# A retention layer with a token and channel mixer on one core: batch 0 multiplies q with its states by row halves, one more transpose of batch 1 goes by crossbar, and k and q are scaled later behind their loads

## The chip, the cores and the metric

The program runs on one NeuronCore of a Trainium2 chip. The metric is device time in microseconds (us) of one launch; the median of three launches of the kernel before is 186.17 us (186.22, 186.17 and 185.26). The engines are TensorE (PE; its weight loads are listed as PEld), VectorE (DVE), ScalarE (ACT), GpSimd (POOL) and SyncE (SP). Each takes its instructions strictly in order.

## What is computed

Two layers follow each other for 4 batches, 768 tokens and 512 channels (8 heads of 64). The first is a recurrent retention with one decay per head, the second a mixer over tokens and then over channels.

```python
for t in range(S):                                   # S = 768, D = 64, H = 8, B = 4
    state = gamma * state + k[:, :, t] (outer) v[:, :, t]
    y[:, :, t] = scale * q[:, :, t] @ state
x  = y as (B, S, H * D)
u  = x + (relu(x^T @ w_tok1) @ w_tok2)^T             # 768 -> 256 -> 768, over tokens
out = u + relu(u @ w_ch1) @ w_ch2                    # 512 -> 1536 -> 512, over channels
```

Inputs and output are float32; inside, the products take float16 and sum in float32.

## The kernel before

The recurrence is done in chunks of 128 tokens (6 chunks). Two heads make a *pair*, so a batch has 4 pairs, and 128 partitions hold the 2 x 64 channels of a pair.

**Front, `front(b, p)`, once for each batch and pair.** k, q and v are loaded by GpSimd's DMA queue (L493, L490), which casts to float16. `decayed` (L531 on ACT, L533 on DVE) multiplies k, and from batch 1 also q, with its decays, one head at a time. `turn` brings k and q into the layout with channels on partitions: by TensorE (L555, L557) and a copy out of PSUM (L565, L570), or by a DMA transpose that SyncE issues (L545), called the crossbar here. The string `TURNS` has three letters for each batch and pair, for k, q and u: `t` is TensorE, `w` is TensorE from a wide load, `x` is the crossbar. The chunk states are k times v (L587), summed over chunks by DVE (L597, L599) and scaled once more into float16 (L617 on ACT, L619 on DVE). Scores are k times q (L638), masked by DVE (L649) and multiplied with v (L669). Then q times the state of the chunk before is added in the same PSUM bank. In the *paired* form (`PAIRED`, all four batches before), the states of both heads lie block-diagonally in a 128 x 128 tile whose other blocks are zero (`cross`, filled by two operations of 64 partitions), and one matmul of 128 rows and 128 columns serves both heads (L695). Here the two PSUM banks hold the two halves of the tokens. The other form, in the code already, keeps the states of a pair in one tile `r`, with head 0 on partitions 0 to 63 and head 1 on 64 to 127, multiplies each head by itself on half of TensorE's rows (L685), and its two PSUM banks hold one head each.

The result is cast to float16 (`x`, L711), goes through the token mixer (L726, relu at L735 or L737, and L746 for the paired form or L751 for the other, which adds to the same banks), is cast again (`u`, L711) and copied in float32 to `X` (L711). u is turned as well, by TensorE (L791, copy at L797) or by the crossbar (L781), into the tile `uT` of its batch.

**Back, `back(b)`, once for each batch.** The channel mixer: batch 0 widens plainly (L825, relu at L841), the others with seven products of half-size blocks instead of eight (L894, with sums on DVE at L864 and L914 and copies at L905). The narrowing (L1047, L1057, L1100 and L973) has copies at L1037 and sums into `X` at L1064 and L982, then stores by SyncE or ScalarE (L1086, L988).

**What sets the order.** The functions only list operations with their dependences. The order in which the engines get them is written down as two tables, `ORDERED` (operation numbers in base 62) and `WAYS` (which of two engines takes it). `arrange` replays that order with a planned cost for each operation, and the replay decides which buffers and PSUM banks an operation gets and how many filler matmuls (L1192) TensorE runs in the first 21 us. An operation's planned costs and its `guard` (a planned distance from what it depends on) therefore act only through the tables and through buffers; at run time an instruction starts when its semaphores allow.

Buffers: 4 each for the loads of k, q and v, so a load waits until the load four before it has been used. GpSimd's queue and SyncE's queue are both first in, first out.

Of the kernel before, what the change touches and what calls it, by code (L numbers as in the profile page):

```python
# [110 lines left out]
def arrange(ops, BANKS, seq, ways):  # L111
# [147 lines left out]
    "0d0106090c070g080e0f000l05031g0a1h0h1k1i1l0j1j0b1u1Q0i1v1w1R1y1U0m1z1S1V1T0k1m1x1n1o0n2u1p1q25241r1B1s0o2q2r"  # L259
    "1t262s0p281A2t1D2v0q30272E29312F1C2G0s1W2I1X321E2H2a1F0u1Y34331Z2J202w212b2x222y0t1G35232z0r2c2d1H2e2A3e2B2f"  # L260
    "1I0w3h2C1L3g2g1J2D1K0v362h2K1M372L2M382N2i390x2O2l3a1N3b3f2P3c4K2j0C3j2Q3d3i3k3m482R0y3l493n3o2k2S3p1O2T2V2m"
    "0A3q1P2n2W2U4a0B3r022o4b2Y3A0z3s2Z3v3t2p3E3u5j3w0F3B4c5k3y3xaf3z4dac3C3FadaP0G3DaM4LaN2Xb1aOb20Daeag3Ob3aQah"
    "3S0EaxaR3RayaY3Qazau3Pav4maw3G4o4e0N3HaZ4f3Iaob03Jb74nb80H4papb93U3KaJ3LaA4g3Mai4h1caqaBaKaC3NaS0IaD4iaE4j1d"
    "aGaFar0Lajas1fak3T3WaL3VaT043XaH4Gal4qaUbd4Hat3Y0MbeaIb41eam3ZanbfaVbm4k4Ibgbo4laW0PbnbhaXb5404J4r18bj0J41b6"
    "bk194244blba0K4s456pbb1a43bq460O1bbObcbi4t4ubrbP4U4vbI0R4M4w4Xbv4N5O4V4x0T5P4O4Pbxbw4Q4y4R4Ybz4SbKbs4T5R4W4z"
    "bt4Cby504Zbp52bB0V5g5fbJ51bA5UbC4A0Q5lbubE4D5m5n4EbTbF4B5obM53bU5V545p5h5W6qc4bX5i5S6rc85q5XbDbN555r5Y47bYbR"
    "5Z56c5c95tbLbS5T6m575v5a5sc7cd5Q585ubV5xce5b5yc65AbWch6n5C5w6o59c07scibZ5z5B0Sc16s4F5Dcm6t6Y6X6u5E0Y5c6v6ZbQ"
    "60cfcn5F6w0U6U61626xcg7t5G6V0W635d5H5J645eca665K676569cj5Icb6b68cc5L6a5M0Xck6c6Acl5N6d156C6y6D706e0Zcq6zcucL"
    "crcvcw6BcM6fcscz6gcQ6EcA6ictcNcRcCcx6hcT71cOcD6GcB6j72cScUcEcJ6l6kd2cV83cG80d0cKcH6WcX7v6F736HcYdRd1136Id3cF"
    "d47u7481dS7y75116Jd78476dWd8dTd5dXdY6Kda7z7wdZdUdbd97A7x6Le07Bdc77e67C6Me1dhbGe7decZbH7Ddie3df85djdd6Ne2e4dk"  # L270
    "78cWcy82d6dA6O7c6QdBe5do796Pdl7bdFdpdC7adGdrcI6R7edmdIdsdqdgdDdJ7d7g6S8y7f10dHdt7hdydKdP7idv14cPdzdLdMdudQdw"
    "7jdEdN16dneWdVeu7k7Eey178zew8B7leXdx86evez7GdOeQ7o877m7JeD8C887HeF7p7IeEeA7r7F7KeH897qeG7nex8A7M7O96eJ8aeBeI"
    "8b7LeS7N8D8e127PeKeM8g7Q6T8c8heU9E8i7ReN8deRf1coe87SeeeVf2c3ea7T998keCec97efeT7U7Wf5eL7Xc28f8m7ZeZ7Ye9ed9ceb"
    "f08E8jeg8F8l7Vf38G9d9a8n9eej9b8H8o9f8Iehf49gf69Fekcpf8ei9h988Jf7en8Kf9eleYePeo8p9Gemfc8Mep8q8L8Q8r8Peq8s8N8u"
    "8t8Ofgfxfdfh9kerfyfl8v9l8SfCfmfefi8w9o8UfDfo9mfnfpfFff8R8T9nfGfzfv8VfjfE9ifqfM8WfA9KfNfsfH9H8Xft9L9jg5fwfJ9I"
    "g6fOfK9J8Yg7ga9MfPg88ZgbfQ8x90fT9q9N9p91fkgdfU929Oge9rfRfW939s9tfVfXgc94fYgkfBg3gf9ug09Pg4gmg1gh9Q9vfZgnggg2"
    "fIglgDgi9wgrfr9SgsgE9A9R9T9x9UgI9ygK9WgJgu9VgofLgLgvgpgt9zgBgMgw9XgFgCgN9ZgSfSgygOgxgTgPgGa19Ya0gzgqhIhCa2hG"
    "gAhE9Ba3hghH9D9ChDhNa4g9gHfuhLhOgjhJhkhMhhhRhKhPgQhFa5gYhQa6hShlhUhigRa8hThrhVgUhphXgV95gZh0a9hshmgWabh1h3hn"
    "hvhoh4esgXhqh5hwh2hth6hjh7huhWh9hxh8aahyhahchYhbi2ijhZi3iRhzikili0i7hBioimi8i4ipa7iqiai1iri5ibi9isiAicihiniH"
    "itiiieivifiCiyiwiBiYhdiSiFizhfiTiDiGiWj8iUiXiIidjfiJiZjriKj0kQiPi6iMj1iQj6iNj3j7jpixigj9ksj4iVjajqkAjdj2jsju"  # L280
    "jektiOjvjbkIjgjtiukJjcjxjhjwjykBjijnj5jzjEjojkiLiEjFjBjlk6jjjAjmkujCkvk2jKk4jDkwk7kKjGkLkxk3kdjIkCkMkekbkykh"
    "jHkzkDkcetjRjLhAjJkffbjSkieOkNjPkgjVkjjQhek5kEkkjTjWfakOkFk8jUkGkPjXjMkHk9kmk0jNkRjYkajOklkSkTknkUkVjZkpkokW"
    "k1kqkXkr"
)
WAYS = (
    "000000000000000000000000000000000000000000000000000000000000000000000000000000010000010000000000000000000100"
    "000001000000010000000000000000000000100001010000010000010000000000000001001001000000000000100000000000000000"
    "001000100000010000010000000001101000000011000000000000000000000000000000000100000100000000000000000000000000"
    "010000000000000000000000000000000000000110010000000000000000000000000001010000000000000000000010000000001101"
    "000100001000000000000000000000100000010000000000000000000000000011001001000000000000000000000000001100000100"  # L290
    "000000000000000000100000000010010000000000000001000000000000001001000000000000000000000000000000000000000000"
    "000000000000000000000000000000000000000000000000000000000000000000000000000011000000000000000000000000000000"
    "000000000000010000000000000000000000000000000010000000000000000100000000010000000001000000100000000010000000"
    "000000000000000000000000000000001100000000000000000000110000000000000000000011000000000000000100101000010000"
    "000001000000101000000000000000000000000100000010100000001000000000000000000000000000000000000000010000000000"
    "000000000011000000000010001000000100000000000000000000000001010000000001000000000000000000000100000010010000"
    "000000010100000000010000001000000000010000000000000001000001000010001000110000010000000100000000000000000000"
    "0000"
# [4 lines left out]
def kernel(  # L303
# [39 lines left out]
    PAIRED = (0, 1, 2, 3,)  # L343
# [3 lines left out]
    TURNS = "twt twt twt twt twx twx twt twt xxx xxx xxx xxx xxx xxx xxx xxx".split()  # L347
# [31 lines left out]
    def one(eng, cost, emit):  # L379
        return [(eng, cost[0], cost[1], emit)]  # L380
# [7 lines left out]
    lnG = const_p.tile([P, H], FP, name="lnG")  # L388
    lnsc = const_p.tile([P, 1], FP, name="lnsc")
# [10 lines left out]
    def prep(eng, cost, emit, deps=(), prio=(-20, 0, -1), takes=(), uses=()):  # L400
        return Op(ops, prio, [(eng, cost, cost + 40, emit)], deps, takes, uses)
# [15 lines left out]
    gy_op = prep("ACT", 190, lambda: nc.scalar.activation(gy, lgs, AF.Exp, bias=lnsc, scale=1.0), [lgs_op])  # L417

# [18 lines left out]
    gq_op = prep("ACT", 2450, emit, [since_op, lnh_op, logs_op], (-20, 0, -1, 1), [LATE], [SINCE])  # L437
# [64 lines left out]
    def front(b, p):  # L502
# [22 lines left out]
        def decayed(tag, src, dep, g, hard):  # L525
            dst, got = Slot(tag), []
            for j in range(2):
                def emit(e, j=j):
# [170 lines left out]
        else:  # L699
            y2 = [op(one("PE", (145, 310), emit), rs + [kt, qt, y0], [], [QT, RS] + Y, tiled="row")]  # L700
# [524 lines left out]
```

## Time and profile before

| | |
|---|---|
| median of three launches | 186.17 us |
| the profiled execution, whole | 186.5 us |
| its span, first to last instruction | 184.7 us |
| TensorE busy | 176.6 us (96%), 2088 matmuls |
| VectorE busy | 168.9 us (91%) |
| ScalarE busy | 137.6 us (74%) |
| granted TensorE clock | 1.000 |
| DMA queue of GpSimd (q0) | 13.18 MB, its packets 91.1% of the 16 engines' span |

The first row of the page gives the span; the time of a launch is that and 1.8 us around it. A row of the timeline is: start, duration, engine, line, operation, output and input names, shapes, and in brackets the idle time before it and what ended that. The shape `128*64 128x64` of a matmul is rows times columns of the weights and then the moving operand. Matmuls are pipelined, so the duration of one matmul is longer than the step from one to the next; the step is read from the starts in the timeline, or from the chain of waits, where `0.67 PE bank L746 x12` is twelve matmuls in 0.67 us. In the rows by windows, each engine has its busy microseconds with the number of instructions, then the granted clock, the number of DMA engine microseconds per microsecond and GB/s.

### The profile page before, as it was taken

To read this page: it belongs to the slowest core of one execution; us is meant where nothing else is said; L and a number is where in the kernel's file an instruction comes from. 1 tells how busy PE (TensorE), PEld (TensorE's weight loads), DVE (VectorE), ACT (ScalarE), POOL (GpSimd) and SP (SyncE) were. 2 spreads that over 40 slices of the span, in tenths; PEclk is the share of its full clock that TensorE was granted. 3 is DMA by queue.
4 is the path that set the end of the run, shared out by engine and by line. 5 is a ranking of instruction groups with operands and counts; after the bars stand their busy time and mean duration, and the time that the engine had idled before them with its cause. 6 is when DMAs were issued, how large, how long until landed. Compare 5 with 4: busy or idle time off the path is not lost.

```text
span 184.7 us, 5303 instructions
## 1 busy us (share of the span) xinstructions
PE 176.6 (96%) x2088; PEld 134.2 (73%) x2088; DVE 168.9 (91%) x446; ACT 137.6 (74%) x323; POOL 53.9 (29%) x63
## 2 busy tenths in 40 slices
PE   7698899999999999999999899999999999999992
PEld 3356698666789988866678798767769986566892
DVE  2799999789999999999999989999999999889993
ACT  5749899857899699999999687798996335786010
POOL 8995776454462108604053200000000000000000
PEclk9999999999999999999999999999999999999999
DMA  6999999999999999999999997604002261100296
GB/s 116 150 164 188 180 185 197 186 197 201 165 157 154 146 157 132 130 153 145 119 224 142 133 253 142 169 0 85 5 0 46 68 188 57 62 0 0 84 378 225
DMA packets 94137, 25.31 MB, mean 137 GB/s; under 512 B 83616, under 2 KB 91296, under 8 KB 94112
## 3 DMA queue, kind: packets, MB, share of 16 engines
q0 software_dynamic: 67728, 13.18, 91.1%
q1 hardware_dynamic: 24944, 9.90, 27.7%
q10 hardware_dynamic: 1440, 1.90, 2.9%
q8 instruction: 16, 0.26, 0.6%
q14 instruction: 9, 0.07, 0.2%
HBM read 26.74 MB, written 6.29 MB: 179 GB/s over the span
## 4 chain that ended last, share of the span: by engine, by line
PE 67%; issue 11%; POOL 11%; DMA 9%; ACTq 0%; ACT 0%; DVE 0%; POOLq 0%
PE bank L894 15%; PE bank L1047 14%; PE bank L1057 9%; PE bank L825 9%; DMA v<-in_v_dram 5%; PE bank L746 4%; DMA k<-in_k_dram 4%; PE bank L726 4%; POOL k L493 3%; PE bank L973 3%; POOL v L493 3%; PE bank L669 2%; PE bank L638 2%; POOL q L490 2%; POOL q L493 2%
## 5 line engine op out<-in xcount | busy, mean ns | idle before, releaser
L649 DVE TENSOR_TENSOR am<-bank,mask 128x384 f16<-128x384 f32 x64 | 32.5, 547 | 1.5 <-PE bank L638 1.3
L914 DVE TENSOR_TENSOR h<-bank,us 128x384 f16<-128x384 f32 x54 | 28.6, 549 | 2.1 <-ACT us L905 1.4
L493 POOL DMA_DIRECT2D v<-in_v_dram x16 | 16.4, 1028 | 38.7 <-PE bank L695 15.1
L905 ACT COPY us<-bank 128x384 f32<-128x384 f32 x50 | 22.9, 483 | 5.3 <-PE bank L894 3.7
L894 PE MATMUL bank<-hs,late 128*128 128x384 f16 x108 | 22.7, 326 | 0.0
L1037 ACT COPY us<-bank 128x256 f32<-128x256 f32 x27 | 10.1, 377 | 14.6 <-PE bank L1047 13.3
L1047 PEld LDWEIGHTS <-hs 128*128 128x128 f16 x192 | 18.1, 98 | 2.9 <-issue 0.8
L1064 DVE TENSOR_TENSOR X<-X,bank 128x256 f32<-128x256 f32 (+1 forms) x45 | 17.8, 407 | 1.4 <-PE bank L1057 1.0
L894 PEld LDWEIGHTS <-late 128*128 128x128 f16 x144 | 13.1, 98 | 7.3 <-DVE hs L864 0.3
L599 DVE SCALAR_TENSOR_TENSOR U<-U,gp,bank 128x64 f32<-128x64 f32 x64 | 16.9, 274 | 0.9 <-ACT U L597 0.2
L1047 PE MATMUL bank<-wsum,hs 128*128 128x256 f16 x132 | 17.6, 273 | 0.0
L825 PE MATMUL bank<-uT,wc 128*128 128x384 f16 x96 | 17.6, 326 | 0.0
L617 ACT ACTIVATE cross<-U,gp 64x320 f16<-64x320 f32 x28 | 15.7, 559 | 2.5 <-DVE U L599 2.0
L493 POOL DMA_DIRECT2D k<-in_k_dram x15 | 15.4, 1029 | 4.0 <-ACT kT L570 2.0
L894 PE MATMUL bank<-uT,wc 128*128 128x384 f16 x72 | 16.5, 326 | 0.0
L711 ACT CAST u<-bank 128x384 f16<-128x384 f32 x28 | 13.4, 482 | 3.3 <-PE bank L746 3.2
L746 PE MATMUL bank<-h,wt 128*128 128x128 f16 x192 | 15.2, 219 | 0.1
L711 ACT COPY X<-bank 128x384 f32<-128x384 f32 x31 | 14.7, 489 | 0.4 <-DVE u L711 0.4
L894 PEld LDWEIGHTS <-wc 128*128 128x128 f16 x108 | 9.9, 98 | 5.7
L726 PE MATMUL bank<-x,wt 128*128 128x128 f16 x192 | 13.4, 219 | 0.6 <-DMA wt<-in_moe_w_tok_dram 0.5
L711 ACT CAST x<-bank 128x384 f16<-128x384 f32 x28 | 13.0, 492 | 1.2 <-PE bank L695 1.2
L746 PEld LDWEIGHTS <-wt 128*128 128x128 f16 x192 | 12.3, 98 | 2.1 <-DMA wt<-in_moe_w_tok_dram 0.2
(94 smaller groups left out, 390.0 us busy)
## 6 DMA issues: line engine op xcount, KB each, us to landing
out_dram<-X SPq DMA_DIRECT2D x16, 256.0 KB, 2.6
q<-in_q_dram POOLq DMA_DIRECT2D x16, 192.0 KB, 8.0
v<-in_v_dram POOLq DMA_DIRECT2D x16, 192.0 KB, 7.9
k<-in_k_dram POOLq DMA_DIRECT2D x15, 192.0 KB, 8.8
wc<-in_moe_w_ch_dram POOLq DMA_DIRECT2D x5, 512.0 KB, 13.8
out_dram<-X ACTq DMA_DIRECT2D x6, 256.0 KB, 2.7
wc<-in_moe_w_ch_dram POOLq DMA_DIRECT2D x2, 256.0 KB, 10.5
us<-in_k_dram SPq DMA_DIRECT2D x1, 384.0 KB, 3.5
```

Source lines behind the costliest of these rows:

```text
L493: (nc.sync if hard else nc.gpsimd).dma_start(out=tile_of(s, [P, 2, NC, D], FP if hard else F16), in_=src.rearrange("h (c p) d -> p (h c) d ...
L599: nc.vector.scalar_tensor_tensor(out=u[:, c], in0=u[:, c - 1], scalar=gp[:, p:p + 1], in1=st, op0=ALU.mult, op1=ALU.add)
L649: nc.vector.tensor_tensor(am, SC[g].tile[:, :m * P].rearrange("p (i t) -> p i t", t=P), mask.to_broadcast([P, m, P]), ALU.mult)
L711: (nc.scalar.copy if e == "ACT" else nc.vector.tensor_copy)(tile(), t)
L726: nc.tensor.matmul(acc[:, jt * P:(jt + 1) * P], wt1[:, i, jt * P:(jt + 1) * P], X16.tile[:, i].rearrange("p h d -> p (h d)"), start=(i == ...
L746: nc.tensor.matmul(Y[j].tile[:, 2 * i * D:2 * (i + 1) * D], wt2[:, jt, t], H1.tile[:, jt], start=False, stop=(jt == NJ - 1), skip_group_ch ...
L825: nc.tensor.matmul(acc[:, :SH], wc1[:, ct, ft * P:(ft + 1) * P], UT.tile[:, ct, sh * SH:(sh + 1) * SH], start=(ct == 0), stop=(ct == NP - 1))
L894: nc.tensor.matmul(acc[:, :SH], left(ct), r[:, ct], start=first and ct == 0, stop=ct == C2 - 1, skip_group_check=True)
L905: (nc.scalar.copy if e == "ACT" else nc.vector.tensor_copy)(ks[:, j], R1.tile[:, :SH])
L914: nc.vector.tensor_tensor(h(m, sh), R.tile[:, :SH], KS.tile[:, j], ALU.add)
L1047: nc.tensor.matmul(acc_[:, lo], l[:, j], r[:, j], start=first and j == 0, stop=j == K2 - 1, skip_group_check=True)
L1064: (nc.vector if e == "DVE" else nc.gpsimd).tensor_tensor(dst(), dst(), b_(), ALU.add)
```

## The change

- `PAIRED` loses batch 0. Its four pairs now take the form with one head per PSUM bank: the states are scaled by one operation of 128 x 320 (`r`, L609 or L611 of the changed file) where two of 64 x 320 stood; q times states is 10 matmuls of 64 rows and 64 columns per pair, on the two halves of the rows, where 5 of 128 rows and 128 columns stood; the second product of the token mixer is 24 matmuls with 64 moving columns per pair where 12 with 128 stood; the casts have the shape 6 x 64 where they had 3 x 128 or 384.
- `TURNS`: u of the third pair of batch 1 goes by the crossbar and not by TensorE.
- `decayed`: the first of the two scalings of k or q of batches 1 to 3 has a planned distance of 1200 ns behind its load.
- ScalarE gets one activation of 128 x 1 (`warm`) ahead of the four that make the decays of q, so its table load moves to this one.
- Two planned costs differ (a DVE scaling of the one float32 k load, q times states by row halves).
- `ORDERED` and `WAYS` are written anew for all of it.

```diff
 ORDERED = (
-    "0d0106090c070g080e0f000l05031g0a1h0h1k1i1l0j1j0b1u1Q0i1v1w1R1y1U0m1z1S1V1T0k1m1x1n1o0n2u1p1q25241r1B1s0o2q2r"
+    "0e0107080d050h090f000g060c031h0m0a0i1l1i0b0n1j1m1k0j1P1v1Q0k1z1T1u1U1R0l1n1S1w1y1o0o2r1x231p222s0p2n1q272o1r"
...
-    PAIRED = (0, 1, 2, 3,)
+    PAIRED = (1, 2, 3,)
...
-    TURNS = "twt twt twt twt twx twx twt twt xxx xxx xxx xxx xxx xxx xxx xxx".split()
+    TURNS = "twt twt twt twt twx twx twx twt xxx xxx xxx xxx xxx xxx xxx xxx".split()
...
+    warm = const_p.tile([P, 1], FP, name="warm")
...
+    warm_op = prep("ACT", 190, lambda: nc.scalar.activation(warm, lnsc, AF.Exp), [logs_op])
...
-    gq_op = prep("ACT", 2450, emit, [since_op, lnh_op, logs_op], (-20, 0, -1, 1), [LATE], [SINCE])
+    gq_op = prep("ACT", 2450, emit, [since_op, lnh_op, logs_op, warm_op], (-20, 0, -1, 1), [LATE], [SINCE])
...
-                got.append(op(either(emit, ACT=(506, 610), DVE=(340, 420) if hard else (600, 690) if b == 0 else (231, 312)),
+                got.append(op(either(emit, ACT=(506, 610), DVE=(580, 660) if hard else (600, 690) if b == 0 else (231, 312)),
                               [dep, gy_op if tag == "q16" else g_op], [] if got else [dst], ([dst] if got else []) + [src],
                               behind=got[-1] if got else None))
+                if b > 0 and j == 0:
+                    got[0].guard = 1200
...
-            y2 = [op(one("PE", (145, 310), emit), rs + [kt, qt, y0], [], [QT, RS] + Y, tiled="row")]
+            y2 = [op(one("PE", (175, 343), emit), rs + [kt, qt, y0], [], [QT, RS] + Y, tiled="row")]
```

Line numbers of the changed file are 2 higher than before for nearly all lines after L417. How the tables move instructions is shown at three places; names with a number are buffers (`k_2162` is a load, `k_22_2299` the scaled copy of it, `bank_...` a PSUM bank).

First, TensorE in batch 0, the pair whose token mixer comes first. Before, one of five matmuls of q with the states and one of twelve of the second product of the mixer:

```order
L695 LDWEIGHTS qT_173
L695 MATMUL bank_298<-cross_77,qT_173 128x128
L746 LDWEIGHTS wt_81
L746 MATMUL bank_328<-h_56_484,wt_81 128x128
```

and now two of ten, one for each head, on TensorE's two row halves:

```order
L687 LDWEIGHTS qT_183
L687 MATMUL bank_323<-r_36_331,qT_183 128x64
L687 LDWEIGHTS qT_183
L687 MATMUL bank_324<-r_36_331,qT_183 128x64
```

The states come from one tile `r` and go to a bank for each head.

Second, SyncE's queue from its first crossbar on, which is in batch 1. Before:

```order
L545 DMA_TRANSPOSE qT_1428<-q_24_1163 128x6x128
L781 DMA_TRANSPOSE uT_1457<-u_62_1141 128x6x128
L545 DMA_TRANSPOSE qT_1490<-q_25_1294 128x6x128
L545 DMA_TRANSPOSE kT_1516<-k_23_1242 128x6x128
L545 DMA_TRANSPOSE kT_1554<-k_21_1498 128x6x128
L781 DMA_TRANSPOSE uT_1457<-u_63_1357 128x6x128
L545 DMA_TRANSPOSE qT_1622<-q_24_1601 128x6x128
L781 DMA_TRANSPOSE uT_1875<-u_61_1827 128x6x128
```

and now:

```order
L547 DMA_TRANSPOSE qT_1477<-q_24_1333 128x6x128
L783 DMA_TRANSPOSE uT_1503<-u_62_1131 128x6x128
L547 DMA_TRANSPOSE kT_1521<-k_23_1398 128x6x128
L547 DMA_TRANSPOSE qT_1549<-q_25_1492 128x6x128
L547 DMA_TRANSPOSE kT_1590<-k_21_1406 128x6x128
L783 DMA_TRANSPOSE uT_1503<-u_63_1438 128x6x128
L783 DMA_TRANSPOSE uT_1503<-u_61_1586 128x6x128
L547 DMA_TRANSPOSE qT_1934<-q_24_1620 128x6x128
```

In the sixth and seventh place stand u of the second and of the third pair of batch 1 (`uT_1503`); the q that stood seventh now comes behind both.

Third, ScalarE in the narrowing of batch 1, where the last loads of k and q are scaled. Before:

```order
L711 COPY X_1848<-bank_2106 128x3x128
L531 ACTIVATE k_22_2299<-k_2162,gk 128x6x64
L1037 COPY us_2211<-bank_2178 128x256
L711 CAST x_55_2341<-bank_2311 128x384
L711 CAST x_55_2341<-bank_2289 128x384
L617 ACTIVATE cross_77<-U_2238,gp 64x5x64
L531 ACTIVATE k_21_2364<-k_2137,gk 128x6x64
```

and now:

```order
L713 COPY X_1910<-bank_2155 128x3x128
L1039 COPY us_2377<-bank_2348 128x256
L531 ACTIVATE k_21_2385<-k_2019,gk 128x6x64
L531 ACTIVATE k_22_2289<-k_1755,gk 128x6x64
L713 CAST x_55_2421<-bank_2361 128x384
L531 ACTIVATE q_25_2427<-q_2236,gy 128x6x64
L713 CAST x_55_2421<-bank_2391 128x384
```

Before, the k load that is scaled here is the third of the last five of GpSimd's queue:

```order
L493 DMA v_2121<-in_v_dram 128x12x64
L493 DMA k_2137<-in_k_dram 128x12x64
L493 DMA k_2162<-in_k_dram 128x12x64
L493 DMA q_2185<-in_q_dram 128x12x64
L493 DMA v_2339<-in_v_dram 128x12x64
```

and now both k loads stand ahead of the v load that opens the last burst, and two q loads follow it:

```order
L493 DMA k_2019<-in_k_dram 128x12x64
L493 DMA v_2195<-in_v_dram 128x12x64
L493 DMA q_2213<-in_q_dram 128x12x64
L493 DMA q_2236<-in_q_dram 128x12x64
L493 DMA v_2418<-in_v_dram 128x12x64
```

So the load that a scaling on ScalarE follows most closely is a k load before (`k_2162`) and a q load now (`q_2236`).

More of the change, by code (lines that the diff above doesn't have):

```diff
@@ new lines @@
+    "0q2p1s251A1t2Z262q1B0r241C2V302B2A2W0u2F1V2C1W2X1D2E0s2Y2t1X1Y2u1E1Z282v29202w212D0w1F2x2y2z2a1G380t2b3b392c"
+    "3a1H0z1K3c1I2d3d1J0x2G1L2H2e2I312J2i0y322f332K343x1M352L2g360D372j3e2h2M3g0A3f2N3t3u3y1N3h2Q0v3i2l2O2k3j2P2R"
+    "0C3v3k2T1O0B3w3l3o3m2m3z4D3A0H3p3n5b452U3q3r2Sa73sa43BaE3C0G4Ea5aHa6a8aF3Da9aI3E0F5caGaTaUaJ3H023Faj0EaV3Jak"
+    "3Iamalan3K3G3Maa41423LaKaoaL460J04ab43ac3Nap44aq0I1daBar3O3PaCaM4f0QaD473Q4jay3Raz484iaW4z4gaX3S1eaY0Nbb3T4h"
+    "bcaAag493U4a4AaZ3V3X4k4bah3Y4c0Kad1gaib04das1fb1aeat3W4BafaN3Z4eb54C0Mb6au19avb7aw4mb80U1baxb9bdaO1abGaP0Lba"
@@ new lines @@
+    "4lb2bH4ob31c574N0Ob44F4P4n4Gbi4R4p0SbeaQaRbfbj4qaSbg0Tbn4H4r4O5Jbk4Ibhbo584S4QbrbAbpbs4J4K4T4vbq4L0PbwbC4M5G"
+    "bt6e5Hbx4Ubl4sbu4W4VbW5d4t5M4XbBbL4u5K4wbm4Y5L5Nbv4xbE5e6h5fc0bM404Z5g5ObP5hc1bXbF5I596i5Pc55i5a5QbQbJ6j5R5j"
+    "bZ50bDbK5l6f5kbN515m6gc6535nbOc97k5o4y5q6P5p5sbSbY5u545rca5tbT0W6k565vbRce6l55bI5w520Rcf5S6mc76n5x0X5T6o5U6p"
+    "c85y5W0V5B5z5Vc25C5X175Z5Y5D61cb5Ac363186062cc5Ec4646scd5F0Z656v6qci1466cjcm6ucDcn6ackcEco6Mcr6N6tcIcs6w6710"
+    "cJcKcpcu68clcLcvcFcMctcB69cw6Q6ScUcN6TcCcy6RcGcP6bczcS6rdL6U6O7lcVcWcQdJ6ccZ6VcTcX6xdK6y7mcA6z6Ad07n0Y7qdM6B"
@@ new lines @@
+    "dO6W7rd26CdN6X15dQdP7scOd17td3dRcq7S7o6Dd4dS7ud97TcYdTd67UdadYdU6EdVd7dZdb7v6Y6F7pdWdc70cH7V6Zds74dgbUdt716I"
+    "6Gdi7Wd8dxdh7X72ddcx73djdydude6H756ddAdkdvdzd5dl77dqdBdX7679dm78dCdn116JdHdrdDdEdo7aeO16cRdIdwdFdf7bem6K12eq"
+    "8qePeo7c7yerdpendG7Y7d8Y7AeveI7Z8rex7z7e8s80ew7g7C7wesep7x6L81ez827heteMey7i7B7jeA7DeB7f83eKeNeE9weubyeC8Z7E"
+    "cgeJ7F8613ch7HeF7G8t90e0eR877IeTe1eS8u7JeD848v88eV7KeU85e68abze27LbV7Oe7eX899291e4e3eWeL7M8c8eeY8w7N94eQ7Peb"
+    "eZ8xe57R8b7Q8dece9958f8y96ef8z8g938Aea97f0e8eged8B988Cf18h99eef48E8ieh9a8j8G8Dei8I8k8H8m8lf88Ffpf5f99cfqejfd"
@@ L299 @@
+    "000100000000000000100000000000000000000000000010000000000000000100001000000100100000000000000001010000100001"
+    "00000010000000000010010000000000001000000000010000000000100010000100000100000001000000010000000000000001"
 )
```

55 lines of the change are left out of this document (18 added, 37 removed).

## The prediction, made before the changed kernel ran

> **What bounds the kernel now.** I read the rows by windows first, to see which engine is full in which stage, then TensorE's waits, then the chain of waits.
>
> ```profile
> 20.00:32.00 12.00, 11.85 (x234) 10.47 (x232) 11.22 (x29) 10.81 (x26) 8.96 (x11) 1.00 1.69 187
> 32.00:52.00 20.00, 20.00 (x207) 13.20 (x205) 18.39 (x36) 15.57 (x36) 9.01 (x10) 1.00 1.74 185
> 76.00:103.00 27.00, 26.90 (x313) 19.62 (x312) 26.77 (x74) 25.86 (x65) 9.05 (x9) 1.00 2.11 155
> 103.00:117.00 14.00, 13.17 (x187) 11.68 (x184) 13.27 (x37) 10.89 (x28) 1.01 (x1) 1.00 0.97 184
> 117.00:151.00 34.00, 34.00 (x366) 26.38 (x365) 32.74 (x81) 25.25 (x63) 0.00 (x0) 1.00 0.25 58
> ```
>
> From 20 us on TensorE (the first busy number) is full in every stage but one: 0.15 us idle from 20 to 32 us, 0.10 from 76 to 103, 0.83 from 103 to 117. So from 20 us the time is TensorE's list of matmuls plus its few waits. From 76 to 103 us VectorE (26.77 of 27) and ScalarE (25.86) are nearly as full: a wait on either there reaches TensorE almost undiminished. What opens that stretch, and its one large wait:
>
> ```profile
> 19.59 0.62 PE L726 MATMUL bank<-x,wt 128*128 128x128 f16 x8 [0.54 <-DMA wt<-in_moe_w_tok_dram]
> 103.23 0.51 PE L638 MATMUL bank<-qT,kT 64*128 64x128 f16 x12
> 104.54 0.81 PE L1047 MATMUL bank<-wc,hs 128*128 128x256 f16 x6 [0.80 <-ACT us L1037]
> 101.26 0.86 ACT L711 COPY X<-bank 128x384 f32<-128x384 f32 x2
> 103.62 0.61 ACT L531 ACTIVATE k<-k,gk 128x384 f16<-128x384 f16 x1 [1.50 <-DMA k<-in_k_dram]
> 104.14 0.35 ACT L1037 COPY us<-bank 128x256 f32<-128x256 f32 x1
> 96.45 7.14 DMA k<-in_k_dram
> ```
>
> The first real product of the token mixer waits for its weights until 19.59 us; before that TensorE runs fillers. At 102.1 us ScalarE has done its copies and stands 1.50 us before a k load that lands at 96.45 + 7.14 = 103.59. Behind it in its queue is the copy L1037 that TensorE's product needs.
>
> **The change part by part, against the span of 184.7 us.** The matmuls, by the steps of the chain:
>
> ```profile
> 29.48 0.67 PE bank L746 x12
> 58.22 0.35 PE bank L669 x12
> 53.15 0.28 PE bank L695 x5
> 53.43 0.44 PE bank L638 x12
> 53.87 0.28 PE bank L587 x10
> 27.13 0.34 PE bank L791 x6
> ```
>
> *Token mixer of batch 0.* Per pair 12 matmuls of 128 columns (0.67 us, 56 ns each) become 24 of 64. The nearest row is L669, the same 128 x 128 weights with 64 columns: 0.35 / 12 = 29 ns, so 0.70 us. Four pairs: 4 x (0.70 - 0.67) = +0.12 us. The bound above is 56 ns each: 4 x 0.67 = +2.7 us; I take the row of the same shape.
>
> *q times states of batch 0.* Five matmuls (0.28 us) become ten of 64 rows and 64 columns on alternating row halves. L638 alternates row halves too: 12 of 128 columns in 0.44 us; if two ran one after the other it would be 12 x 56 = 0.67, so two overlap (0.34) and 0.10 goes to the change of form. Ten of half the columns then take 10 x 29 / 2 + 0.10 = 0.25 us, and L587 (ten on column halves) took 0.28. Without overlap it is 0.29 + 0.10 = 0.39. So the bounds are 4 x (0.25 - 0.28) = -0.1 and 4 x (0.39 - 0.28) = +0.4; I take 0.
>
> [...]
>
> *u of the third pair by crossbar.* TensorE loses six transposes (L791): -0.34 us. A copy of uT leaves ScalarE or VectorE. SyncE gains one transpose, priced below.
>
> *States scaled once.*
>
> ```profile
> L617 ACT ACTIVATE cross<-U,gp 64x320 f16<-64x320 f32 x28 | 15.7, 559 | 2.5 <-DVE U L599 2.0
> L619 DVE TENSOR_SCALAR cross<-U,gp 64x320 f16<-64x320 f32 x4 | 2.2, 540 | 0.1
> L436 ACT ACT_TABLE_LOAD x1 | 1.3, 1283 | 2.2 <-DVE lnh L430 2.2
> ```
>
> An operation's length goes with its elements per partition, so one of 128 x 320 takes about the 0.56 us of one of 64 x 320: four times 0.55 us leave ScalarE and VectorE. In the window from 20 to 32 us they have 11.22 and 10.81 of 12 us of work, but TensorE idles there only 0.15 us, so at most that is won. Against it, the casts x of a pair can now both start only when all ten matmuls are done, where the first half could go ahead; TensorE's list has another pair's matmuls in between (q times states, scores, the mixer of the pair before, over 1 us together) and two casts take 0.9. I count 0, with 0.4 either way.
>
> *Table load.* It waits 2.2 us now; the 128 x 1 activation needs less and pulls it and the decays forward by under 1 us. The weights that land at 19.59 hide that: before them TensorE has the same real matmuls in both lists (four pairs' transposes, three pairs' scores). Without that cover it would be worth under 1 us. Worth 0.
>
> *The margin.* The k load of the wait now stands ahead of the last burst in GpSimd's queue and is long there, and its scaling is not followed by TensorE's next copy. The gap at TensorE goes: L638 starts at 103.23 and needs 0.44, the next product at 104.54, so -0.87 us.
>
> *What may be late next.* In-order ScalarE and SyncE now stand before other transfers. The rows that price them:
>
> ```profile
> 69.49 1.28 SPq L781 DMA_TRANSPOSE uT<-u  x1
> 70.88 1.28 SPq L545 DMA_TRANSPOSE qT<-q  x1
> uT<-u SPq DMA_TRANSPOSE x1, 5.7
> qT<-q SPq DMA_TRANSPOSE x1, 7.4
> 69.82 1.09 POOL L493 DMA_DIRECT2D v<-in_v_dram  x1 [8.92 <-PE bank L587]
> 70.90 2.04 POOL L493 DMA_DIRECT2D q<-in_q_dram  x2
> q<-in_q_dram POOLq DMA_DIRECT2D x1, 192.0 KB, 7.7
> k<-in_k_dram POOLq DMA_DIRECT2D x1, 192.0 KB, 9.2
> 77.39 1.19 PE L894 MATMUL bank<-uT,wc 128*128 128x384 f16 x6
> 94.44 1.01 POOL L493 DMA_DIRECT2D v<-in_v_dram  x1 [8.37 <-PE bank L695]
> 97.56 1.03 POOL L493 DMA_DIRECT2D q<-in_q_dram  x1
> ```
>
> (a) The widening of batch 1 needs all of uT. The third pair's u is cast on ScalarE behind two scalings, by my count of the list at 69.4 us; its crossbar goes out at 69.5, where the one of 69.49 took 5.7 us: it lands at 75.2. TensorE's first product of that widening came at 77.39; six transposes (0.34) fewer and ten matmuls of another pair (0.28) that now follow it make that about 76.8. Cover 1.6 us; behind the product stand all of TensorE's matmuls. If it goes out one crossbar later (70.8) and takes 7.4 us, it lands at 78.2 and costs 1.4; with the 9.2 us of the slowest load of that burst, 3.2.
> (b) In the burst of loads that starts at 69.82 the second is now a k whose scaling stands behind two copies of that widening (turn about 78.0). A second load took 7.7 us from 70.90, to 78.6: 0.6 us late. But the transposes that shared the DMA engines then ran until 70.88 + 7.4 = 78.3, and SyncE now has none in that place until about 80 us. I take on time.
> (c) The last burst: v at about 95.0, then two q, the second at 97.1, landing by the k's 7.14 us at 104.2; ScalarE's turn comes behind the cast of x after 104.1, at 104.5. Between 0 and the old 0.9 us.
> Together 0 to 0.6 + 0.9 with (a) in cover, up to 4.7 if all are late; I take +0.1, since each has cover, if little.
>
> *Sum.* 184.7 + 0.12 + 0 - 0.34 + 0 - 0.87 + 0.1 = 183.7 us of span. With the 1.8 us around it, 185.5 against the profiled 186.5; that execution was 0.3 above the median of 186.17, so I forecast **185.2 us**.
>
> **Rivals.**
> *B, the wait only moves.* ScalarE stands before the second q of the last burst, (c), or the k of (b), and loses the 0.9 us again: 185.2 + 0.9 = 186.1. For it: cover of 0.3 us and less, and a burst of loads still opens when a v buffer comes free. Against it: the load that decides has the v and one q ahead of it and no k, and ScalarE's turn is by my count behind its landing.
> *C, the third u comes late (slower).* The crossbar between 67 and 78 us now carries k, u, u with the loads of batch 2 in flight; TensorE stands still before L894. Price 1.4 to 3.2; between the two, landing at 78.9, 2.1: 185.2 + 2.1 = 187.3. It decides from 76.8 us on; below that it costs nothing, and at about 77.8 it has eaten the gain. For it: 5.7 and 7.4 us side by side in the rows. Against it: the slower one shared with q and v loads as well as a transpose ahead.
> *D, a fixed price per matmul.* If the 64-column matmuls of batch 0 step at 56 ns, +2.6 to the sum: 187.8. L669 speaks against it.
> *E, the order does more.* What I count at 0 comes in: 0.4 at the casts of batch 0, 0.1 at q times states, the 0.25 us of idle time before 103 us, and nothing is late (0.1): 185.2 - 0.85 = 184.3.
>
> **Chances.** Forecast 0.52 (0.36 of it faster by over 0.5%, 0.16 within), B 0.21 (0.02 faster, 0.18 within, 0.01 slower), C 0.17 (0.01 within, 0.16 slower), D 0.03 (slower), E 0.07 (faster). So faster 0.45, within 0.5% 0.35, slower 0.20; 0.5% is 0.93 us, about what a measurement of this kernel tells from no change. The range of 8 in 10 goes from just below E, 184.2, to C's 187.3; the forecast's own is 184.6 to 185.9.
>
> **What would show it.** Right: batch 0's mixer step (24 matmuls) 0.70 us and q times states 0.25 to 0.28; TensorE's first product of the mixer still at 19.6 after the weights; no idle over 0.3 us at the copies L1039 around 104 us; the crossbar of the third u landed before TensorE's first L896 (L894 before); k loads of batch 3 long there when ScalarE reaches them. Wrong: TensorE idle at L896 with a DMA of uT as what ended it (C), ScalarE idle before L531 on q or k by a DMA (B), steps of 50 ns and more at L753 (D), or a wait in a place that I haven't priced, as batch 0's casts.

## The result, and the profile after

Six launches of the changed kernel took 188.92 us in the median (188.71 to 189.24), six of the kernel before on the same chip 185.48 (185.26 to 186.22): a ratio of 1.017, 95% interval 1.014 to 1.019. The change makes the kernel 3.4 us slower where 185.2 us, a little faster, was forecast. The profiled launch took 189.0 us with a span of 187.2.

The first row of the page on the engines, for the changed kernel:

```profile
PE 178.1 (95%) x2151; PEld 134.3 (72%) x2151; DVE 170.5 (91%) x447; ACT 134.7 (72%) x318; POOL 53.5 (29%) x63
```

TensorE has 2151 matmuls where it had 2088: 68 more in batch 0, six transposes fewer, one filler more. Its rows by windows (columns as before: TensorE, its weight loads, VectorE, ScalarE and GpSimd busy, clock, DMA share, GB/s):

```profile
20.00:32.00 12.00, 10.26 (x263) 9.03 (x261) 9.70 (x23) 8.89 (x22) 9.25 (x11) 1.00 1.65 189
32.00:52.00 20.00, 20.00 (x224) 13.59 (x224) 17.26 (x36) 14.49 (x34) 10.52 (x11) 1.00 1.78 184
76.00:103.00 27.00, 26.37 (x302) 18.39 (x300) 26.76 (x73) 26.03 (x65) 9.62 (x10) 1.00 1.90 159
103.00:117.00 14.00, 14.00 (x189) 12.60 (x187) 13.93 (x40) 11.58 (x29) 1.01 (x1) 1.00 1.25 205
```

The list of TensorE's waits from 20 to 184 us (us in total, times, longest):

```profile
PE bank L557 <- issue: 1.0, 1, 1.0
PE bank L728 <- issue: 0.8, 1, 0.8
PE bank L640 <- DVE X L1066: 0.4, 1, 0.4
```

The hole of 0.83 us at 103 to 117 us is gone, as forecast. A new one stands from 20 to 32 us: 10.26 us busy of 12, where it was 11.85, although more matmuls run there (263 against 234). VectorE and ScalarE are less busy there than before (9.70 and 8.89 against 11.22 and 10.81), so neither is the bound, and TensorE's two waits have the releaser "issue": it stood for nothing that the profile names. The timeline shows where:

```profile
19.40 0.84 PE L728 MATMUL bank<-x,wt 128*128 128x128 f16 x12 [0.33 <-DMA wt<-in_moe_w_tok_dram]
23.51 0.87 PE L753 MATMUL bank<-h,wt 128*128 128x64 f16 x24
24.31 0.53 PE L557 MATMUL bank<-ident,q 128*64 128x128 f16 x12
24.77 0.34 PE L728 MATMUL bank<-x,wt 128*128 128x128 f16 x3
25.89 0.68 PE L728 MATMUL bank<-x,wt 128*128 128x128 f16 x9 [0.78 <-issue]
26.68 0.32 PE L687 MATMUL bank<-r,qT 64*128 64x64 f16 x10
26.93 0.35 PE L663 MATMUL bank<-v,am 128*128 128x64 f16 x6
...
30.80 0.23 PE L557 MATMUL bank<-ident,q 128*64 128x128 f16 x2
31.98 1.14 PE L557 MATMUL bank<-ident,q 128*64 128x128 f16 x34 [0.96 <-issue]
```

Both stands are in the middle of a series of equal matmuls, after the 3rd of 12 products and the 2nd of 36 transposes, which have no semaphore between them. Counted in TensorE's instructions (each matmul is a weight load and a product), the 706th and the 962nd come first after a stand: 256 apart. The page has two rows of packets that carry instructions. One (q14) has 9 packets of at most 8 KB. The other, of the kernel before and then of the changed one (queue, packets, MB, share of the 16 engines):

```profile
q8 instruction: 16, 0.26, 0.6%
```

```profile
q8 instruction: 17, 0.28, 0.6%
```

Each of these packets is 16,384 bytes in the trace. Putting a border at instruction 193 + 256 n, so that both stands fall on one, there are 16 borders in the 4,190 instructions of the kernel before and 17 in the 4,317 of the changed one: a packet for each border. Read from the trace (us):

```
kernel    border   first instruction   its packet   later by   block before     stand at
          at no.   behind it starts    starts                  it used up in    the border
before     449        20.71             23.67        2.96         8.54             -
before     705        27.41             30.19        2.78         6.70             -
before     961        35.84             38.24        2.40         8.43             -
changed    449        20.18             23.52        3.34         8.78             -
changed    705        25.89             29.51        3.62         5.71            0.99
changed    961        31.98             35.82        3.84         6.09            1.18
```

The stand is counted here from the start of the last matmul ahead of the border to the start of the first one behind it. A packet takes 0.9 to 1.0 us here. I read this so: in these stages the next block of instructions is asked for when TensorE enters the present one, and its transfer starts 2.4 to 3.8 us later. The trace shows the packet and not the asking; late in the program, with few loads (DMA share 0.25 from 117 to 151 us), some packets of the changed kernel start up to 1.3 us before the first instruction behind their border does (148.44 against 149.73), so the asking may be somewhat earlier than the entry. Where TensorE stands, it goes on 1.5 us behind the end of the packet (23.52 + 0.89 = 24.41, then 25.89; 29.51 + 0.89 = 30.40, then 31.98), 5.7 and 6.1 us after it entered the block before. In the thirteen stands of 0.5 us and more of the changed kernel and the runs below, the 1.5 us are 1.2 to 1.6. The kernel before used its blocks up in 6.70 us and more and never noticed. The changed one needs 4.7 and 4.9 us (5.71 less 0.99, 6.09 less 1.18) and stands for the rest. This is theory F.

**Where the 3.6 us of span are.** For each matmul I take its start less the place it would have if TensorE never waited (steps of 29, 56, 110 and 163 ns for 64, 128, 256 and 384 columns, from 0.35 us for twelve in L669, 0.67 for twelve in L746, 0.66 for six in L1047 and 1.95 for twelve in L825 in the chain of the kernel before; half of it on row and column halves, where L638 has 0.44 for twelve and L587 0.28 for ten; 0.1 us at a change of form, an estimate from L638; all from the first token product on). TensorE's lag behind its list, in us:

```
                              at 33   77     92    103    134   end
before, run again  (E1)        0.56  0.93   1.38   1.40   1.47  1.47
changed                        2.40  2.86   3.55   4.50   4.74  4.82
t2 of batch 0 in halves (E2)   1.69  2.14   3.01   3.08   3.12  3.12
changed, batch 0 paired (E4)   0.78  1.24   1.95   2.88   3.15  3.20
before, batch 0 unpaired (E7)  2.23  2.77   3.25   3.70   3.71  3.73
changed, exchange (E9)         2.37  2.80   3.55   4.47   4.71  4.79
changed, fillers cut (E12)     1.57  2.05   2.75   3.68   3.96  4.01
```

Changed against before: 1.84 us more up to 33 us, 0.33 from there to 92, 0.93 from 92 to 103, 0.25 behind: 3.35 in all. The list itself is 0.29 us shorter (159.02 against 159.31), it starts 0.15 later, and the time behind the last matmul is 0.40 longer: 3.61 us, the 187.2 against 183.6 of span. The steps are round prices: with 0.1 us at every change of the rows or columns of the weights, the four shares are 1.97, 0.34, 0.94 and 0.24 us and the list is 0.44 us shorter, so the split is good to some 0.15 us. The 0.33 and the 0.25 us were not taken apart.

### The profile page after: what moved, and what is told of

It is laid out like the page before. It is cut to its first block, busy times and chain, and to the rows that moved or that the text cites. A ratio compares the mean times of both kernels' runs of the same rounds, so it can differ in the third digit from the quotient of the medians.

```text
span 187.2 us, 5429 instructions
## 1 busy us (share of the span) xinstructions
PE 178.1 (95%) x2151; PEld 134.3 (72%) x2151; DVE 170.5 (91%) x447; ACT 134.7 (72%) x318; POOL 53.5 (29%) x63
## 3 DMA queue, kind: packets, MB, share of 16 engines
q10 hardware_dynamic: 1440, 2.23, 3.3%
## 4 chain that ended last, share of the span: by engine, by line
PE 81%; POOL 5%; DMA 5%; DVE 4%; issue 2%; ACT 2%; POOLq 0%; DVEq 0%
PE bank L896 20%; PE bank L1049 15%; PE bank L1059 11%; PE bank L827 8%; PE bank L728 5%; DMA wt<-in_moe_w_tok_dram 5%; PE bank L748 4%; PE bank L640 3%; PE bank L975 3%; PE bank L671 2%; PE bank L697 2%; PE bank L753 2%; POOL k L493 2%; PE bank L589 2%; POOL q L490 2%
## 5 line engine op out<-in xcount | busy, mean ns | idle before, releaser
L907 ACT COPY us<-bank 128x384 f32<-128x384 f32 x51 | 23.4, 485 | 8.3 <-PE bank L896 4.7
L1039 ACT COPY us<-bank 128x256 f32<-128x256 f32 x26 | 9.6, 374 | 11.5 <-PE bank L1049 10.2
L713 ACT CAST x<-bank 128x384 f16<-128x384 f32 x31 | 14.7, 492 | 1.2 <-PE bank L697 1.0
L843 ACT ACTIVATE h<-bank 128x384 f16<-128x384 f32 x24 | 11.0, 486 | 4.5 <-PE bank L827 4.4
L1059 PEld LDWEIGHTS <-h 128*128 128x128 f16 x132 | 12.5, 98 | 1.8
L713 ACT COPY X<-bank 128x384 f32<-128x384 f32 x28 | 13.5, 495 | 0.3 <-DVE u L713 0.3
L728 PEld LDWEIGHTS <-wt 128*128 128x128 f16 x192 | 11.7, 98 | 2.6 <-issue 0.9
```

The lines of the kernel that those rows point to most:

```text
L713: (nc.scalar.copy if e == "ACT" else nc.vector.tensor_copy)(tile(), t)
L728: nc.tensor.matmul(acc[:, jt * P:(jt + 1) * P], wt1[:, i, jt * P:(jt + 1) * P], X16.tile[:, i].rearrange("p h d -> p (h d)"), start=(i == ...
L907: (nc.scalar.copy if e == "ACT" else nc.vector.tensor_copy)(ks[:, j], R1.tile[:, :SH])
L1059: nc.tensor.matmul(acc_[:, lo], l[:, j], r[:, j], start=first and j == 0, stop=j == K2 - 1, skip_group_check=True)
```

## The experiments

All times are medians beside runs of the kernel before on the same chip. F is the theory above; the other letters are named in the expectations, and B to E in the prediction (rival E is not one of the runs E1 to E12).

**E1, the kernel before once more.**

> The kernel before, unchanged, profiled once more. The forecast took 0.87 us out for a wait at 103.2 to 104.5 us that stood in the one profiled execution (186.5 us); the median of six executions of this kernel is 185.48. Theory W (the wait belongs to the kernel): it is there again, near 0.8 us, and the span is 184.7. Rival (the wait is an accident of that execution): it is missing or shorter, the span is near 183.7 to 184.0, and removing it was worth little from the start.

185.36 us, span 183.6, and no wait of TensorE over 0.2 us from 20 us on. ScalarE in that execution:

```profile
100.94 0.86 ACT L711 COPY X<-bank 128x384 f32<-128x384 f32 x2
102.00 0.61 ACT L531 ACTIVATE k<-k,gk 128x384 f16<-128x384 f16 x1 [0.20 <-DMA k<-in_k_dram]
102.52 0.35 ACT L1037 COPY us<-bank 128x256 f32<-128x256 f32 x1
```

The k load landed at 102.0 us, not at 103.59; the copy L1037 behind the scaling came at 102.52, not at 104.14, and the 0.87 us are not there. The rival holds: the wait comes and goes with the landing of one load.

**E2, instructions alone, in the kernel before.**

```diff
                     for jt in range(NJ):
-                        nc.tensor.matmul(Y[j].tile[:, 2 * i * D:2 * (i + 1) * D], wt2[:, jt, t], H1.tile[:, jt],
-                                         start=False, stop=(jt == NJ - 1), skip_group_check=True)
+                        for g in range(2 if b == 0 else 1):
+                            c0, c1 = (g * D, (g + 1) * D) if b == 0 else (0, 2 * D)
+                            nc.tensor.matmul(Y[j].tile[:, 2 * i * D + c0:2 * i * D + c1], wt2[:, jt, t],
+                                             H1.tile[:, jt, c0:c1], start=False, stop=(jt == NJ - 1),
+                                             skip_group_check=True)
```

> The kernel before with one edit: the second token product of batch 0 as 96 matmuls of 64 columns where 48 of 128 stand, same banks, same result. Theory F (TensorE's instructions arrive in blocks of 256, a block every 6 us or so while the loads run): the blocks that the kernel before uses up in 6.70 us are then used up in some 5.4 to 5.8 us, so TensorE stands at two places between 24 and 34 us, for nothing that the profile names, 256 instructions apart, and the time rises by 0.6 to 1.8 us. Rival P (the price list of the forecast: 29 ns for 64 columns): plus 0.1 us, no stand. Rival D (a fixed price of 56 ns for a small matmul): plus 2.6 us, spread over the 96 matmuls, no stand.

187.64 us against 186.33, ratio 1.009 (1.005 to 1.013). One stand, not two, at instruction 961:

```profile
30.20 1.14 PE L555 MATMUL bank<-ident,q 128*64 128x128 f16 x34
32.32 0.25 PE L555 MATMUL bank<-ident,q 128*64 128x128 f16 x2 [0.97 <-issue]
```

The 48 more matmuls cost a stand of 1.1 us at transposes that the edit doesn't touch; the block before the border at 705 took 5.46 us and just came through. F holds; P and D fall. The trace also has a wait of 0.5 us for a v load at 79 us, so not all of the 1.3 us over the kernel before is the stand.

**E3, E12, the borders moved by 32 matmuls of zeros.** The fillers ahead of the data are cut in three, the first 16 of 37 in E3, the last 16 in E12.

```diff
-                    nc.tensor.matmul(spare[:, :384], zero[:, :P], zero, start=True, stop=True)
+                    cut = 3 if fills >= SHIFT else 1
+                    fills += 1
+                    for g in range(cut):
+                        c0, c1 = g * 384 // cut, (g + 1) * 384 // cut
+                        nc.tensor.matmul(spare[:, c0:c1], zero[:, :P], zero[:, c0:c1], start=True, stop=True)
```

> The changed kernel with one edit: 16 of the matmuls of zeros that keep TensorE busy before the data comes are cut into three of 128 columns each, 32 matmuls or 64 instructions more, all before 20 us. Theory F (blocks of 256 instructions): the borders of the blocks fall 64 instructions earlier in the program, the first of the two stands (at 25.1 us) goes, the second comes 64 instructions earlier and takes some 0.7 us, and the kernel is 1.1 to 1.5 us faster than the change, at 187.4 to 187.8 us. Rival S (the stands belong to their places: these matmuls, their banks or their tiles): both stay, the time stays at 188.9 us. Rival P (every instruction has its price): 188.9 or more.

E3: 187.81 us against 186.33, ratio 1.0095 (1.0057 to 1.0132), so less over before than the change. Both stands left their places and came at two second token products (L753), 0.5 and 1.2 us, at the moved borders. The blocks took 6.3 and 6.4 us to come, so the first stand shrank and didn't go; and TensorE reached the first token product at 20.51 us, 1.1 late: of the early transposes, six of k took 0.85 us (0.49 in the change) and twelve of q 0.85 (0.77), behind a wait for a q load of 0.76 (0.27).

> The changed kernel with the last 16 of its matmuls of zeros (all between 11 and 20 us, where TensorE waits for data) cut into three of 128 columns each, 32 matmuls or 64 instructions more; nothing else. In the run that cut the first 16, TensorE came to the first token product 1.1 us later, since its early transposes ran slowly. Theory F: with fetches of 6.0 us the borders fall 64 instructions earlier, the stand at 25.1 us goes, one stand of about 0.7 us comes near 29 to 30 us, TensorE is 1.0 to 1.3 us behind its list at 33 us where the change was 2.26 to 2.40, and the time is 1.0 to 1.4 us under the change (ratio to before 1.010 to 1.012 where the change has 1.0167 and 1.0175). If the fetches take 6.3 us, as in the run that cut the first 16, there are two stands of together 1.4 to 1.6 us, and the gain is 0.5 us. Rival S (the stands belong to their places in the program): no change, ratio 1.017.

E12: 187.66 us against 186.34, ratio 1.0078 (1.0059 to 1.0097). Its waits:

```profile
PE bank L753 <- issue: 1.0, 1, 1.0
PE bank L640 <- DVE X L1066: 0.4, 1, 0.4
```

One stand, in another place (30.21 us; the border is there; at the border before, only 0.14 us over a step), and 32 *more* matmuls halve what the change costs. No theory that only gives each instruction a price can say that; S falls too. The size was between the two that I gave: one stand, but of 1.1 us.

**E4, the change without its batch 0.** `PAIRED = (0, 1, 2, 3,)` in the changed kernel; the second operation on the states stands in the tables behind the first.

> The changed kernel with batch 0 paired again, as in the kernel before: states scaled by two operations, q with its states by 20 whole matmuls, the second token product by 48. The other parts of the change stay: third u by crossbar, the early table load, the new order. Theory F: 68 matmuls fewer in batch 0, so the blocks last over 6 us, the two stands go, and the time falls by 1.6 to 2.0 us to 186.9 to 187.3. The rest above the forecast (0.9 us between 92 and 107 us) stays, since it belongs to the order. Rival O (the order is at fault for all of it): it stays within 0.4 us of 188.9.

187.37 us against 186.33, ratio 1.0079 (1.0052 to 1.0106). No stand without a name; lag at 33 us 0.78 instead of 2.40, of which 0.74 is a wait of my own making (q with the states, for the second operation on VectorE). F holds for the 1.84 us. From 92 to 103 us the lag grows by 0.93 as in the change, so that is the rest of the change.

**E5, the changed kernel once more.**

> The changed kernel once more, beside the kernels of this call on one chip. Theory F (TensorE gets its instructions in blocks of 256): the two stands come again at the same two instructions, near 25 and 31 us, together about 2 us. If they are an accident of one execution, they move or go. Time 188.4 to 189.5 us.

189.55 us against 186.37, ratio 1.0175 (1.0146 to 1.0203); stands of 0.7 and 1.0 us at the same two instructions; the time is 0.05 us over what was expected.

**E6, the loads held back.**

```diff
         def emit():
+            for _ in range(160 if key == "c1" and "c1" not in wops_seen else 0):
+                nc.gpsimd.iota(junk, pattern=[[1, 8]], base=0, channel_multiplier=0,
+                               allow_small_or_imprecise_dtypes=True)
+            wops_seen.add(key)
             nc.gpsimd.dma_start(out=dst, in_=src.rearrange("(i p) j -> p i j", p=P))
```

> The changed kernel with one edit: ahead of the first load of the channel weights GpSimd writes a tile of 8 columns 160 times, which holds back every load behind it for some 7 us from 22 us on, so that the loads in flight run dry at about 27 us. The total time will be longer, since the loads come late, and says nothing; what counts are the two stands. Theory F with the loads as the cause of the slow fetch: the first stand (25.1 to 25.9 us) stays, since its block was asked for at 20 us with the queues full; the packet of instructions after it starts under 2 us behind the border of its block where it took 3.6 us, and the second stand (1.1 us) shrinks below 0.3 us or goes. Rival (the fetch takes 6 us whatever the loads do): the second stand stays at 1.1 us.

The writes held the loads for longer than meant (the kernel took 218.59 us). The DMA engines ran dry at 28 us, the last but one column:

```profile
24.00:28.00 4.00, 3.42 (x92) 3.01 (x88) 3.53 (x10) 3.02 (x9) 2.77 (x19) 1.00 1.63 177
28.00:32.00 4.00, 4.00 (x111) 3.86 (x108) 2.80 (x7) 3.38 (x8) 2.64 (x20) 1.00 0.08 14
```

and TensorE's timeline at the two borders:

```profile
25.75 0.68 PE L733 MATMUL bank<-x,wt 128*128 128x128 f16 x9 [0.57 <-issue]
30.65 1.18 PE L562 MATMUL bank<-ident,q 128*64 128x128 f16 x36
```

The first stand is there, the second is gone: all 36 transposes run through, TensorE is busy 4.00 of 4 us. The packet of the border at 25.74 us started 1.89 us behind it (3.62 in the change), the next 0.39 behind its own (3.84). So the fetch is slow with the loads here: 3.62 and 3.84 us with the queues full, 0.39 where the DMA share is 0.08; this rests on one execution.

**E7, E8, two parts of the change alone, in the kernel before.** E7: `PAIRED = (1, 2, 3,)`, tables merged (in the first pair, two of TensorE's operations had to change places, and the casts of x of all four moved). E8: the seventh word of `TURNS` is `twx`, the crossbar where the copy stood.

> The kernel before with only batch 0 unpaired, in the order of the kernel before: states scaled by one operation, q with its states by row halves, second token product in 64 columns; 68 matmuls more, no crossbar, no new order, no margin. Theory F: one or two stands 256 instructions apart between 24 and 33 us, plus 1.0 to 2.4 us against before. Rival P (price list): plus 0.1 us. Rival O (the new order is what costs): within 0.4 us of before.

188.60 us against 186.37, ratio 1.0137 (1.0100 to 1.0173). Stands of 0.6 and 1.1 us at instructions 705 and 961:

```profile
26.57 0.72 PE L724 MATMUL bank<-x,wt 128*128 128x128 f16 x10 [0.44 <-issue]
32.77 0.86 PE L553 MATMUL bank<-ident,q 128*64 128x128 f16 x24 [0.90 <-ACT k L529]
```

The second is put down to a scaling of k that happened to end at 32.53 us; these are transposes of q in the middle of a series, and the border is there. Batch 0 alone brings most of the loss, without the new order: F holds, P and O fall.

> The kernel before with only the u of the third pair of batch 1 by crossbar: six transposes and a copy fewer, one crossbar transpose more, the order otherwise as before. The forecast: minus 0.34 us of TensorE list, no new wait, so 0.2 to 0.4 us faster than before. Rival C (u late by crossbar): a wait at the channel products of batch 1 near 70 to 77 us, plus 0.5 to 2 us.

192.38 us against 186.37, ratio 1.032 (1.030 to 1.035):

```profile
72.31 16.10 SPq L781 DMA_TRANSPOSE uT<-u  x2
...
81.62 0.82 PE L894 MATMUL bank<-uT,wc 128*128 128x384 f16 x2 [3.29 <-DMA uT<-u]
```

Rival C's wait, but with the order of the kernel before: the crossbar of the third u, in the place of its copy, comes too late there. The wait is not the whole price. The windows behind it have the granted clock of TensorE, the last column but two, at 0.50 and 0.65:

```profile
80.00:84.00 4.00, 2.38 (x12) 1.53 (x13) 2.30 (x5) 0.72 (x2) 0.00 (x0) 0.50 2.75 154
84.00:88.00 4.00, 4.00 (x27) 2.44 (x25) 1.79 (x5) 2.87 (x9) 0.00 (x0) 0.65 0.74 35
```

So a stop of 3.3 us was followed by matmuls at about half speed (six of L746 step in 0.64 us, 82.24 to 82.88, against 0.34 in the chain of the kernel before), while the clock stayed at 1.00 through the stands of about 1 us in the changed kernel (1.00 from 20 to 32 us). The run says nothing of the changed kernel's order, where both of the last crossbars of u go out from 70.17 us on, the widening starts at 78.52, and nothing waits.

**E9, E10, the loss at 100 us.** The changed kernel by windows, then VectorE's timeline at 100 us, then TensorE's:

```profile
92.00:97.00 5.00, 5.00 (x59) 3.36 (x54) 4.92 (x15) 4.80 (x13) 0.19 (x1) 1.00 1.27 209
97.00:103.00 6.00, 5.52 (x72) 4.26 (x71) 5.97 (x16) 5.81 (x16) 2.85 (x3) 1.00 1.59 108
```

```profile
99.47 0.54 DVE L1013 TENSOR_TENSOR hs<-h 128x768 f16<-128x768 f16 x1
99.93 0.41 DVE L1066 TENSOR_TENSOR X<-X,bank 128x256 f32<-128x256 f32 x1
100.26 0.55 DVE L1013 TENSOR_TENSOR hs<-h,h 128x768 f16<-128x768 f16 x1
```

```profile
99.59 0.39 PE L640 MATMUL bank<-qT,kT 64*128 64x128 f16 x7
100.39 0.32 PE L640 MATMUL bank<-qT,kT 64*128 64x128 f16 x5 [0.41 <-DVE X L1066]
```

The scores wait for a bank that the addition into X frees at 100.34, behind a sum of h that is needed later. E9 exchanges the two:

```diff
-L1013 TENSOR_TENSOR hs_2233<-h_67_1845 128x768
 L1066 TENSOR_TENSOR X_1170<-X_1170,bank_2206 128x256
+L1013 TENSOR_TENSOR hs_2244<-h_67_1845 128x768
```

> The changed kernel with two neighbours of VectorE's list exchanged, at 99.5 us: the addition into X that reads a bank of the scores goes ahead of a sum of h (0.46 us) that stood before it. Theory Q (0.6 us of the loss at 100 us is the scores waiting for a bank that VectorE, busy without a pause from 92 to 103 us, frees late): the wait of 0.41 us and the 0.19 beside it go, TensorE falls behind its list there by 0.3 us instead of 0.9, and the kernel is 0.3 to 0.6 us faster than the change (189.0 to 189.2 where the change has 189.55). Rival (the 0.6 us come back at the next wait, since VectorE is the bound of this stretch): within 0.2 us of the change.

189.07 us against 186.30, ratio 1.0164 (1.0130 to 1.0197), no less than the change. The wait of the scores is gone, and:

```profile
101.26 0.83 PE L1049 MATMUL bank<-wsum,hs 128*128 128x256 f16 x6 [0.52 <-DVE hs L1013]
```

The lag at 103 us is 4.47 instead of 4.50. The rival holds: the wait on VectorE of 0.41 us that was taken away came back as 0.52 at the next product that needs VectorE. That VectorE is full does not explain the 0.93 us, though. In the kernel before (E1) it is as full, and TensorE doesn't wait:

```profile
97.00:103.00 6.00, 6.00 (x90) 5.20 (x90) 6.00 (x18) 5.63 (x15) 1.27 (x2) 1.00 2.11 152
```

E10 is E4 with that exchange and the second operation on the states on the other engine than the first.

> The changed kernel with batch 0 paired again, the second of the two operations that scale the states of each pair on the engine that the first isn't on (it stood 0.74 us in the run with both on one), and the exchange on VectorE at 99.5 us. By the sum of what the traces show: 187.37 minus 0.6 to 0.74 minus 0.3 to 0.6, so 186.0 to 186.5, level with the kernel before (186.3 on this chip). If it is over 187, waits that nothing here names come back.

188.44 us against 186.30, ratio 1.0127 (1.0100 to 1.0154): a miss. The scaling that moved to VectorE held up the masks of the scores (1.0 us at 22.5 us), and the 0.9 at 100 us stayed.

**E11, the wait at 103 us taken out of the kernel before.**

```diff
-L531 ACTIVATE k_22_2299<-k_2162,gk 128x6x64
 L1037 COPY us_2211<-bank_2178 128x256
+L531 ACTIVATE k_22_2307<-k_2162,gk 128x6x64
```

> The kernel before with two neighbours of ScalarE's list exchanged at 102 us: the copy that TensorE waited for (0.87 us in the first profiled execution, none in the second) goes ahead of the scaling of a k that stands until its load lands (103.59 us in the one, 102.0 in the other). Theory V (the landing of that load differs from execution to execution, and is most of the spread of 185.3 to 186.8 us between them): the median falls by 0.3 to 0.8 us and the spread shrinks to half. Rival (the spread is from elsewhere): median and spread as before, or 0.2 to 0.4 us slower, since the scaled k comes 0.35 us later.

185.80 us (185.37 to 186.48, 12 launches) against 186.30 (185.45 to 187.55, 17), ratio 0.9985 (0.9963 to 1.0007): not told from no change. The launches still fall into two groups, near 185.6 and 186.4, so the landing of that load is not most of the spread. Four of the five near 186.4 have a granted clock of 0.991, the seven near 185.6 have 0.998 or 1.000; what lowers it no run shows. No version that I ran is shown to beat the kernel before.

## Why the prediction was wrong

*What bounds the kernel.* "From 20 us the time is TensorE's list of matmuls plus its few waits" was true of the kernel before and is the step that failed for the change. It has a second condition in these runs: that the instructions are there. The changed TensorE stood 0.99 and 1.18 us at two borders where they were not, and the prediction had no term for that. The row of instruction packets stood on the page and was not read. With the times of the borders it would have shown blocks of 6.70 us (6.41 in E1) and packets that end 3.3 to 3.9 us behind their border. That 1.5 us more pass until TensorE goes on shows only where it stands, so the size could not have been read off before, but the resource could.

*Token mixer and q times states of batch 0, +0.12 and 0.* Each by itself came near: the 24 matmuls step in 0.80 us (23.51 to 24.31), 0.1 over my 0.70, q with the states in 0.25. As instructions the 68 matmuls are 136 more, in a stretch whose tightest block, 6.41 to 6.70 us, had only 0.3 to 1.0 us to spare against the 5.7 and 6.1 us that a block took to come in the changed kernel. The term should have been +1.84. Batch 0 alone in the old order (E7) has 1.67 (2.23 less 0.56), and 48 of the 68 matmuls alone (E2) have 1.13. A price for each added matmul doesn't give it either: E12 has 32 matmuls more than the change and is faster (1.0078 over before against 1.0167).

*The margin, -0.87.* The wait went, but E1 shows that it was a late load in one execution; the median had little of it. It was subtracted from an execution that had it and then carried over to a median.

*What may be late next, +0.1.* (a) The third u was in time, and rival C did not come; E8 shows that this was the order's doing. (b) and (c): no wait for a load is left at TensorE. Rival B's price came true with another mechanism: 0.93 us between 92 and 103 us, where VectorE has hardly a pause (and had none before). It is in every kernel with the new order (changed, E4, E9, E10, E12) and not in those with the old (E1, E2; E7 has 0.45). So it belongs to the order; which of the moved operations makes VectorE late was not settled.

*States scaled once, 0.* On ScalarE one operation of 128 x 320 took 562 ns in the changed kernel, as one of 64 x 320 did (559 before). On VectorE it took 386 where one of 64 x 320 took 540, so the length was not the same for the same elements per partition there.

*The rest.* -0.34 for the transposes with +0.12 is -0.22: the list is 0.29 to 0.44 shorter. It is added up from nearly the prices of the forecast, so this tests the count of matmuls more than the prices. The first token product starts with the landing of its weights (19.40), so the table load was worth nothing. Rivals D and E fell.

## What to carry to other kernels

An engine that is "full" needs its instructions brought to it; in the changed kernel TensorE stood 0.99 and 1.18 us for them. Count the instructions of each dense stretch, and compare the time that a block of them (256 here) lasts with the time that a block takes to come (5.7 and 6.1 us in the changed kernel). That is the time from a border to the end of the stand at the next one, or, where nothing stands, to the end of the packet and (here) some 1.5 us more. Here, with the queues full of loads, a matmul may not last under about 47 ns in the mean (an estimate from the 5.7 and 6.1 us: 6 us for 128 of them), so halving the columns of a matmul of 56 ns was free only in the list. A stand in the middle of a series, with "issue" (0.78 and 0.96 us in the changed kernel) or an unlikely releaser (0.90 us in E7), was the sign of this here; it moved (E3, E12) when instructions were added ahead of it in the program. And a wait is subtracted only if a second execution has it.

## What the runs showed of the hardware that I had not expected

The page counts the instruction packets (q8, 0.6%) on the same 16 DMA engines as the loads (q0, 91.1% in the kernel before), and the fetch went with the loads: 2.4 to 4.1 us from border to packet between 20 and 36 us in all runs with the loads on (2.4 to 3.8 in the two kernels above), 0.39 us without (E6), and mostly under 1 us behind 95 us. Fillers that only keep TensorE busy are part of the program's length, and 64 instructions of zeros more brought the time from 1.7% over the kernel before to 0.8% (E12).
